# Linear attention, then a squared-ReLU MLP, on one core: diagonal sums on VectorE and GpSimd, state terms as row tiles, another order

## The chip, the core and the metric

The kernel runs on one core of one Trainium2 chip. The core has a matrix engine (TensorE, PE in the profile; PEld are its weight loads), VectorE (DVE), ScalarE (ACT), GpSimd (POOL) and SyncE (SP, which here only issues DMAs). Matrix products land in PSUM, 8 banks of 128 x 512 f32; operands lie in SBUF. The metric is the device time of one execution in microseconds, the median of several runs.

## The reference

For 4 batches, 8 heads, 768 positions and a head size of 48:

```
for t in range(S):
    cur = einsum('bhd,bhe->bhde', u * k[t], v[t])
    y[t] = einsum('bhd,bhde->bhe', r[t], state + cur)
    state = w * state + einsum('bhd,bhe->bhde', k[t], v[t])
x = y.transpose(0, 2, 1, 3).reshape(3072, 384)
out = relu(x @ w_in) ** 2 @ w_out        # 384 -> 2048 -> 384
```

## The kernel before, in words

**Units.** The 768 positions are cut into 6 chunks of 128. A unit is one chunk of one batch, all 8 heads: 24 units, numbered so that units 4c to 4c + 3 are chunk c of the four batches. Heads go in 4 pairs; a pair is 2 x 48 columns, padded to 2 x 64 where it is turned.

**Attention of a unit.** `load` brings r, k and v (192 KB each, in `ldr`, `ldk`, `ldv`). `scale` (DVE) multiplies r with rising and k with falling powers of w into `rkw`, so that decay inside the chunk becomes a plain product. `turn` (PE, with `evict_rk` on ACT, units 0 to 5) or `turn_dma` (a DMA transpose, units 6 on) gives `rkT`. `at` computes k^T q for every head in two PSUM banks, the two heads of a pair on partitions 0 to 63 and 64 to 127 of the array; `ats` does it for two units (four banks). `mask` (DVE) applies the triangle and writes `am`. `y_mm` multiplies `am` with v (8 matmuls) and adds r times the state (4 matmuls with the state `stb`, in which the two heads of a pair stand in a block-diagonal 128 x 96 with zeros elsewhere). The position's own term, the sum over d of r u k, times v, is the diagonal: `rk` (DVE) multiplies the turned r and k, `sums` contracts the product with `uwb` on PE (4 matmuls of 8 columns), `diag_v` (DVE) multiplies the sums with v, and `evict_y` (DVE) adds that to y.

**State.** `sums` also forms k^T v (4 matmuls). `state_add` adds it to `st32`, `state_decay` multiplies with the decay of a chunk, both DVE; `state_cast` (ACT) writes the bf16 copy `stb`, in two halves. Chunk 5 needs no new state.

**MLP.** y goes turned (`x_turn` and `evict_x`, or `x_dma`) into `xT`; `mm1` computes a slice of the hidden layer for one or two units (12 or 6 matmuls), `relu` on ACT, `square` on ACT or DVE, `mm2` a quarter of the second product (4 matmuls of 384 columns), `evict_o` and `store`. The last unit's product goes in two halves (`mm2_half`).

**Order.** A text, `SCHEDULE`, lists every step; each engine works its own instructions in that order. `@` gives the PSUM banks that a step takes, `name:unit:...` its arguments; the last field of `square` is 1 for ACT and 0 for DVE; `load` and `store` name the queue. `fill` is a matmul on constants whose result nobody reads. `SP` also issues both kinds of transposing DMA.

Lines that are named below: 233 fill, 288 scale, 311 turn, 320 rk, 328 at, 340 mask, 348 diagonal sums, 353 state sums, 362 diag_v, 370 to 376 state, 382 state_cast, 391 and 397 y, 406 evict_y, 421 x_turn, 435 mm1, 443 relu, 452 and 454 square, 461 mm2, 476 halves, 260 the small chain of products on GpSimd in the head.

Of the kernel before, what the change touches and what calls it, by code (L numbers as in the profile page):

```python
# [26 lines left out]
2*fill:256@7 fill:256@2 evict_y:0 fill:256@2 wout:1:0 mm1:1:1:1@7 state_add:0 x_turn:0@2 load:4:kt:POOL mm1:1:1:0@6  # L27
mask:2:1 evict_x:0 relu:1:1:1 state_add:1 mm1:0:1:0@3 relu:1:1:0 mm1:0:1:1@1 mask:2:0 square:1:1:1:1 scale:3:1
relu:0:1:0 4*fill:256@7 square:1:1:0:0 fill:256@7 cast_v:2 3*fill:256@7 state_cast:1 fill:256@7 square:0:1:0:0
sums:2@2 wout:2:0 y_mm:2@0 mm1:0:1:2@7 relu:0:1:1 diag_v:2 evict_y:2 mm1:1:1:2@4 load:4:vt:POOL load:6:kt:SP scale:3:0  # L30
x_turn:2@6 turn:3:1@5 state_add:2 evict_x:2 turn:3:0@3 fill:256@0 evict_rk:3:1 fill:256@0 square:0:1:1:0 mm1:2:1:2@1
evict_rk:3:0 wout:3:0 mm1:2:1:0@0 relu:1:1:2 rk:3 relu:0:1:2 at:3@6,2 load:5:vt:POOL relu:2:1:0 mm1:2:1:1@5 mask:3:1
cast_v:3 mm1:1:1:3@3 square:2:1:0:0 relu:2:1:1 mask:3:0 mm1:2:1:3@4 square:1:1:2:1 square:2:1:1:1 mm1:0:1:3@7
scale:4:0 relu:2:1:2 mm2:1:0@0 relu:1:1:3 scale:5:0 sums:3@2 relu:0:1:3 y_mm:3@5 turn:4:0@6 diag_v:3 square:2:1:2:1
mm2:0:0@1 square:0:1:2:1 evict_y:3 mm2:2:0@3 state_add:3 evict_rk:4:0 mm2:1:1 state_cast:0 scale:4:1 x_turn:3@7
square:0:1:3:0 relu:2:1:3 mm2:0:1 evict_x:3 square:1:1:3:0 turn:4:1@5 mm2:2:1 evict_rk:4:1 load:9:kt:SP mm1:3:1:1@6
cast_v:4 rk:4 at:4@2,4 relu:3:1:1 load:7:kt:SP mm1:3:1:0@7 mask:4:1 square:2:1:3:1 mm2:1:2 mask:4:0 relu:3:1:0
# [10 lines left out]
relu:5:1:3 load:8:vt:SP evict_o:2 sums:7@0 mask:7:0 load:11:kt:SP mm2:4:1 relu:5:1:1 rk:8 load:11:rt:SP store:2:POOL
relu:5:1:2 mm2:4:2 diag_v:7 store:3:POOL state_add:7 y_mm:7@1 store:0:POOL mm2:4:3 scale:10:1 store:1:POOL mm1:6:1:0@7
evict_y:7 square:5:1:2:0 x_dma:7 mm1:6:1:1@3 relu:6:1:0 state_decay:7 mm2:5:0@4 square:5:1:1:0 square:6:1:0:1  # L50
load:11:vt:SP square:5:1:3:1 ats:8@6,5,0,1 load:12:kt:SP relu:6:1:1 mm2:6:0@7 mask:8:0 mm1:6:1:3@3 rk:9 scale:10:0
mm1:6:1:2@6 mask:9:0 relu:6:1:3 turn_dma:10 mm2:5:1 mask:9:1 relu:6:1:2 sums:9@3 cast_v:8 mask:8:1 y_mm:9@0
# [20 lines left out]
mask:14:0 load:18:kt:SP mm2:10:3 mask:15:1 mm1:12:2:3@5 mask:14:1 turn_dma:16 mask:15:0 mm1:12:2:1@6 relu:12:2:3
scale:17:0 mm1:12:2:5@7 cast_v:15 load:16:vt:SP scale:17:1 square:12:2:3:1 mm1:12:2:0@4 turn_dma:17 mm2:11:2
relu:12:2:0 y_mm:15@3 relu:12:2:5 load:17:vt:SP sums:15@5 relu:12:2:1 sums:14@4 state_add:15 mm1:12:2:7@7
square:12:2:1:1 diag_v:14 mm1:12:2:2@6 evict_o:8 diag_v:15 square:12:2:0:1 mm1:12:2:6@0 relu:12:2:7 evict_y:15
# [41 lines left out]
def kernel(  # L118
# [13 lines left out]
    C = 128  # L132
# [148 lines left out]
    def pair(x):  # L281
        return x.rearrange("p (a o) d -> p a o d", o=2)
# [263 lines left out]
```

## Time and profile before

| | |
|---|---|
| median of 3 runs | 173.61 us (173.19 to 174.07) |
| the execution profiled | 173.05 us, of which the span 171.3 |
| PE busy | 164.8 us (96%), 1931 matmuls |
| DVE busy | 138.0 us (81%) |
| ACT busy | 120.8 us (71%) |
| POOL busy | 30.5 us (18%), nearly all issuing DMAs |

The span is what the instructions cover; the rest of a time lies around it. A matmul's record is longer than its share of the pipeline (an `mm2` matmul shows 326 ns and the next starts 163 ns later), so PE work is read here from starts, in the chain of waits. Rows of a group read: line, engine, operation, output and input, count, then busy time and mean ns of one, then idle time before them. Rows of a timeline or chain begin with start and length in us.

### The profile page before, as it was taken

How to read it: one execution, taken by the hardware profiler on the slowest of the kernel's cores; microseconds unless marked ns; L12 is line 12 of the kernel's file. 1: busy time of each engine (PE TensorE's matmuls, PEld its weight loads, DVE VectorE, ACT ScalarE, POOL GpSimd, SP SyncE). 2: the span in 40 equal slices, each digit the busy share in tenths (PEclk: the TensorE clock that was granted, in tenths of full speed). 3: DMA queues.
4: the chain of work that ended last, by engine and by line, in shares of the span. 5: the costliest groups of instructions: out<-in, count | busy, mean ns of one | idle time of the engine just before them, and what ended most of it. 6: DMA issues, size and time to landing. Idle time of an engine off the chain costs nothing.

```text
span 171.3 us, 4810 instructions
## 1 busy us (share of the span) xinstructions
PE 164.8 (96%) x1931; PEld 132.1 (77%) x1931; DVE 138.0 (81%) x298; ACT 120.8 (71%) x252; POOL 30.5 (18%) x62
## 2 busy tenths in 40 slices
PE   7949999999999999999999999999999999999993
PEld 3637998787887788697796896896898776999662
DVE  5457997879999999999989879988989797764800
ACT  4533669999699547788599599499359986295830
POOL 8989440000002200000300000303000030030010
PEclk9987999999999999999999999999999999999999
DMA  5999999989996999899999999999959994150014
GB/s 106 199 212 213 220 249 244 222 157 158 187 169 120 286 145 169 166 186 148 238 229 123 182 186 128 254 149 204 262 97 211 201 150 134 32 161 0 4 62 168
DMA packets 94784, 28.83 MB, mean 168 GB/s; under 512 B 90665, under 2 KB 92714, under 8 KB 94762
## 3 DMA queue, kind: packets, MB, share of 16 engines
q1 hardware_dynamic: 90512, 19.08, 71.8%
q0 software_dynamic: 4224, 9.44, 21.1%
q8 instruction: 15, 0.25, 0.6%
q14 instruction: 7, 0.06, 0.1%
q10 hardware_dynamic: 26, 0.00, 0.0%
HBM read 20.45 MB, written 4.72 MB: 147 GB/s over the span
## 4 chain that ended last, share of the span: by engine, by line
PE 87%; DVE 5%; DMA 4%; POOL 2%; issue 1%; POOLq 0%; DVEq 0%
PE bank L461 35%; PE bank L435 35%; DMA ldr<-in_r_dram 4%; PE bank L328 4%; PE bank L391 3%; PE bank L353 2%; PE bank L397 2%; PE bank L476 2%; PE bank L233 1%; PE bank L311 1%; PE bank L348 1%; DVE yb L406 1%; DVE am L340 1%; DVE st L370 1%; PE bank L421 1%
## 5 line engine op out<-in xcount | busy, mean ns | idle before, releaser
L443 ACT ACTIVATE gr<-bank 128x512 f32<-128x512 f32 x96 | 53.8, 603 | 27.8 <-PE bank L435 24.4
L435 PE MATMUL bank<-xT,w_in_q 128*128 128x128 bf16 (+1 forms) x768 | 70.6, 246 | 0.0
L461 PE MATMUL bank<-w_out_q,g 128*128 128x384 bf16 x368 | 67.6, 326 | 0.0
L435 PEld LDWEIGHTS <-w_in_q 128*128 128x128 bf16 x768 | 64.1, 113 | 2.4
L461 PEld LDWEIGHTS <-g 128*128 128x128 bf16 x368 | 34.0, 98 | 18.9 <-ACT g L452 0.5
L454 DVE TENSOR_TENSOR g<-gr 128x512 bf16<-128x512 f32 x50 | 33.0, 686 | 6.5 <-ACT gr L443 6.4
L495 POOL DMA_DIRECT2D out_dram<-osb x21 | 11.3, 543 | 130.3 <-ACT osb L468 119.6
L340 DVE TENSOR_TENSOR am<-bank,smask 128x512 bf16<-128x512 f32 x48 | 30.8, 684 | 3.5 <-PE bank L328 3.2
L452 ACT ACTIVATE g<-gr 128x512 bf16<-128x512 f32 x46 | 28.2, 633 | 0.5
L406 DVE TENSOR_TENSOR yb<-bank,dv 128x384 bf16<-128x384 f32 x24 | 13.3, 556 | 3.9 <-PE bank L391 1.2
L288 DVE TENSOR_TENSOR rkw<-ldr,wpos 128x384 bf16<-128x384 f32 x24 | 12.9, 552 | 3.8 <-ACT wpos L241 2.2
L382 ACT CAST stb<-st 64x192 bf16<-64x192 f32 x40 | 13.9, 348 | 2.2 <-DVE st L376 1.9
L362 DVE TENSOR_TENSOR dv<-vb,bank 128x384 f32<-128x384 bf16 x24 | 13.0, 549 | 2.9 <-PE bank L353 2.1
L288 DVE TENSOR_TENSOR rkw<-ldk,wneg 128x384 bf16<-128x384 f32 x24 | 13.1, 552 | 0.6 <-DMA ldk<-in_k_dram 0.5
L292 ACT CAST vb<-ldv 128x384 bf16<-128x384 f32 x24 | 12.2, 512 | 0.6 <-DMA ldv<-in_v_dram 0.4
L468 ACT COPY osb<-bank 128x384 f32<-128x384 f32 x23 | 10.6, 481 | 2.7 <-PE bank L461 2.7
L372 DVE TENSOR_TENSOR st<-bank,st 64x192 f32<-64x192 f32 x32 | 11.3, 352 | 1.3 <-PE bank L353 1.0
L320 DVE TENSOR_TENSOR rk<-rkT 128x512 bf16<-128x512 bf16 x24 | 10.1, 419 | 1.9 <-ACT rkT L315 1.4
L233 PE MATMUL bank<-warm 128*128 128x256 bf16 x53 | 10.0, 336 | 1.2 <-DVE warm L179 1.2
L315 ACT COPY rkT<-bank 128x512 bf16<-128x512 bf16 x12 | 6.6, 591 | 4.1 <-PE bank L311 4.0
L328 PEld LDWEIGHTS <-rkT 64*128 64x128 bf16 x192 | 5.6, 95 | 4.6 <-issue 4.4
L328 PE MATMUL bank<-rkT 64*128 64x128 bf16 x192 | 8.1, 220 | 0.8 <-ACT rkT L315 0.8
(58 smaller groups left out, 112.6 us busy)
## 6 DMA issues: line engine op xcount, KB each, us to landing
ldk<-in_k_dram SPq DMA_DIRECT2D x22, 192.0 KB, 4.3
out_dram<-osb POOLq DMA_DIRECT2D x21, 192.0 KB, 3.5
ldr<-in_r_dram SPq DMA_DIRECT2D x20, 192.0 KB, 4.3
ldv<-in_v_dram SPq DMA_DIRECT2D x19, 192.0 KB, 4.5
w_in_q<-in_moe_w_in_dram POOLq DMA_DIRECT2D x4, 384.0 KB, 9.6
w_out_q<-in_moe_w_out_dram POOLq DMA_DIRECT2D x4, 384.0 KB, 10.8
ldv<-in_v_dram POOLq DMA_DIRECT2D x5, 192.0 KB, 9.6
ldr<-in_r_dram POOLq DMA_DIRECT2D x4, 192.0 KB, 8.9
```

Of the source, the lines that this page charges most:

```text
L288: nc.vector.tensor_tensor(t["rkw"][:, x, :, :, :D], pair(src), pair(wx), ALU.mult)
L292: nc.scalar.copy(tiles[i]["vb"], tiles[i]["vt"])
L328: nc.tensor.matmul(out=t["at"][o][:, p, :], lhsT=t["rkT"][sl, 1, p, :], rhs=t["rkT"][sl, 0, p, :], start=True, stop=True,)
L340: nc.vector.tensor_tensor(am, t["at"][o], smask.unsqueeze(1).to_broadcast([C, HP, C]), ALU.mult)
L362: nc.vector.tensor_tensor(t["dv"], t["vb"], t["d"].unsqueeze(2).to_broadcast([C, H, D]), ALU.mult)
L382: nc.scalar.copy(stb[b][sl, :, o * D : (o + 1) * D], st32[b][sl])
L406: nc.vector.tensor_tensor(t["yb"], t["y"], t["dv"].rearrange("p h d -> p (h d)"), ALU.add)
L435: nc.tensor.matmul(out=t["h", s][:, a], lhsT=turned, rhs=chunks[c]["xT"][:, n, b : b + m, :], start=(n == 0), stop=(n == NK - 1),)
L443: nc.scalar.activation(t["gr", s], t["h", s], AF.Relu)
L452: nc.scalar.activation(g, x, AF.Square)
L454: nc.vector.tensor_tensor(g, x, x, ALU.mult)
L461: nc.tensor.matmul(out=t["o"], lhsT=chunks[units[i][0]]["g"][:, f, units[i][1], :], rhs=w_out_q[f // 4][:, f % 4, :], start=(f == 0), stop ...
```

## The change

From unit 8 on, three things are computed in another way, and the whole order is another one.

1. **Diagonal sums.** Instead of `rk` and 4 matmuls, `product` (DVE) multiplies r and k before they are turned, `weigh` (POOL) multiplies by w u, laid out over all partitions by two loads and one product that stand around the steps of units 7 and 8, two `fold`s (POOL) add halves of the 48 columns to 24 and 12, and `head_sums` (DVE) reduces the last 12.
2. **y from the state.** `ats` is followed by 8 matmuls per unit, one a head, with 64 rows each, that use the state as it is (`stc`, one cast from unit 4 on) and write each head's half of y: one bank for the even heads of both units, one for the odd. `ys` later adds `am` times v for both units.
3. **evict_y** reads the two banks, in two instructions.

```
+    def wide_load(x):
+        src = (w, u)[x].rearrange("h d -> (h d)").unsqueeze(0).to_broadcast([128, dm])
+        nc.sync.dma_start(out=wide[x].rearrange("p h d -> p (h d)"), in_=src)
+    def wide_product():
+        nc.gpsimd.tensor_tensor(wide[1], wide[1], wide[0], ALU.mult)
+    def product(i):
+        t["pr"] = buffer("pr", [C, H, D], BF16)
+        nc.vector.tensor_tensor(pair(t["pr"]), t["rkw"][:, 0, :, :, :D], t["rkw"][:, 1, :, :, :D], ALU.mult)
+    def weigh(i):
+        t["pw"] = buffer("pw", [C, H, D], F32)
+        nc.gpsimd.tensor_tensor(t["pw"], t["pr"], wide[1], ALU.mult)
+    def fold(i, n):
+        x = tiles[i]["pw"]
+        m = D >> (n + 1)
+        nc.gpsimd.tensor_tensor(x[:, :, :m], x[:, :, :m], x[:, :, m : 2 * m], ALU.add)
+    def head_sums(i):
+        t["d"] = buffer("ds", [C, H], F32)
+        nc.vector.tensor_reduce(out=t["d"], in_=t["pw"][:, :, : D // 4], axis=mybir.AxisListType.X, op=ALU.add)
+    def halves(i):
+        return [bank("y", i - i % 2, o).rearrange("p (u x) -> p u x", u=2)[:, i % 2, : dm // 2].rearrange("p (a d) -> p a d", a=HP) for o in range(2)]
     def ats(i):
         at(i)
         at(i + 1)
+        for j in (i, i + 1):
+            y = halves(j)
+            for p in range(HP):
+                for o in range(2):
+                    sl = slice(o * 64, o * 64 + 64)
+                    nc.tensor.matmul(
+                        out=y[o][:, p, :], lhsT=tiles[j]["rkT"][sl, 0, p, :], rhs=stc[units[j][1]][sl, p, :],
+                        start=(j == i and p == 0), stop=False, skip_group_check=True,
+                    )
...
-        for p in range(HP):
+        for p in range(HP if i < WIDE_FROM else 0):
...
-        for o in range(2):
+        if i >= WIDE_FROM - B:
+            nc.scalar.copy(stc[b], st32[b])
+        for o in range(2 if i < WIDE_FROM - B else 0):
...
+    def ys(i):
+        for j in (i, i + 1):
+            for p in range(HP):
+                for o in range(2):
+                    nc.tensor.matmul(
+                        out=y[o][:, p, :], lhsT=t[f"am{o}"][:, p, :], rhs=t["vb"][:, 2 * p + o, :],
+                        start=False, stop=j > i and p == HP - 1, skip_group_check=True,
+                    )
...
+        if i >= WIDE_FROM:
+            for o, y in enumerate(halves(i)):
+                nc.vector.tensor_tensor(out_y[:, o], y, dv[:, o], ALU.add)
+            return
```

The order, from its start to the first `mm1` step, before and after:

```
-load:1:kt:SP fill:256@7 load:0:rt:SP 2*fill:256@7 load:0:kt:SP 2*fill:256@7 load:1:rt:POOL 2*fill:256@7 load:2:kt:SP
-2*fill:256@7 columns:0 columns:1 load:1:vt:POOL spread_log@0 load:2:vt:SP load:2:rt:POOL load:5:rt:SP fill:256@7
-power:0 win:0:0 2*fill:256@7 power:1 fill:256@7 scale:0:0 fill:256@7 load:0:vt:POOL fill:256@7 scale:1:1 2*fill:256@7
-turn:1:1@1 win:1:0 scale:0:1 turn:0:0@2 evict_rk:1:1 load:3:kt:POOL scale:1:0 turn:0:1@3 load:5:kt:SP evict_rk:0:0
-turn:1:0@4 evict_rk:0:1 win:2:0 spread_columns@5 evict_rk:1:0 rk:0 load:3:rt:POOL cast_v:1 rk:1 at:1@6,7 copy_columns
-at:0@0,1 u_columns scale:2:0 fill:256@5 scale:2:1 fill:256@5 end_columns turn:2:0@2 fill:256@5 mask:0:0 turn:2:1@3
-evict_rk:2:0 sums:1@4 mask:0:1 evict_rk:2:1 3*fill:256@5 2*fill:256@2 mask:1:0 at:2@5,0 win:3:0 2*fill:256@3 mask:1:1
-2*fill:256@3 fill:256@6 cast_v:0 load:3:vt:POOL 2*fill:256@6 diag_v:1 fill:256@6 y_mm:1@2 y_mm:0@3 load:6:rt:SP
-sums:0@1 evict_y:1 wout:0:0 2*fill:256@7 rk:2 fill:256@7 load:4:rt:POOL x_turn:1@6 diag_v:0 2*fill:256@7 evict_x:1
...
+load:0:rt:SP fill@7 load:1:kt:SP 3*fill@7 load:0:kt:SP load:1:rt:POOL load:2:kt:SP columns:0 columns:1 load:2:rt:POOL
+spread_log@0 load:2:vt:SP load:1:vt:POOL load:5:rt:SP fill@7 power:1 win:1:0 power:0 load:0:vt:POOL scale:0:0
+scale:1:1 win:0:0 load:5:kt:SP turn:1:1@1 load:3:kt:POOL scale:0:1 turn:0:1@2 win:2:0 turn:0:0@3 evict_rk:0:1 fill@0
+load:3:rt:POOL fill@0 evict_rk:1:1 fill@0 scale:2:0 fill@2 evict_rk:0:0 fill@2 scale:1:0 spread_columns@4 scale:2:1
+fill@3 rk:0 turn:2:0@5 turn:1:0@6 2*fill@3 evict_rk:1:0 fill@3 at:0@7,0 evict_rk:2:0 rk:1 at:1@2,1 mask:0:0 cast_v:1
+turn:2:1@3 fill@6 fill@5 evict_rk:2:1 fill@5 copy_columns mask:0:1 u_columns at:2@6,5 mask:1:1 win:3:0 cast_v:0
+sums:1@7 mask:1:0 cast_v:2 end_columns diag_v:1 y_mm:1@4 sums:0@3 rk:2 y_mm:0@0 evict_y:1 diag_v:0 x_turn:1@1 fill@4
...
```

One stretch of the steady part, after:

```
+store:7:POOL evict_o:6 square:8:2:4:0 load:15:vt:SP ats:12@6,0,1,4,3,2 square:8:2:5:0 scale:15:1 mm2:9:2 mask:12:0
+weigh:13 turn_dma:15 mm2:8:2 mask:13:1 mm1:10:2:0@6 fold:13:0 load:16:kt:SP scale:14:0 mm1:10:2:4@4 relu:10:2:0
+fold:12:0 mask:12:1 square:8:2:6:1 mm1:10:2:5@6 turn_dma:14 fold:12:1 mask:13:0 relu:10:2:4 store:5:POOL mm1:10:2:3@0
+head_sums:12 square:8:2:7:1 state_decay:11 fold:13:1 mm1:10:2:1@1 cast_v:13 load:17:rt:SP head_sums:13 product:14
+mm1:10:2:7@4 diag_v:12 relu:10:2:1 state_decay:10 ys:12 square:10:2:0:1 diag_v:13 mm2:8:3 state_cast:11 evict_y:12
```

The new order has 14 fills between the first `mm1` and the steps of unit 10, and one in the tail; the old one has 11 after the first `mm1`, all before unit 4. Squares: 50 on DVE and 46 on ACT before, 37 and 59 after.

More of the change, by code (lines that the diff above doesn't have):

```diff
@@ L28 @@
[L28 to L37, printed above, removed]
@@ L48 @@
[L48 to L52, printed above, removed]
@@ L73 @@
[L73 to L76, printed above, removed]
-mm1:12:2:4@5 relu:12:2:2 state_decay:12 x_dma:15 square:12:2:7:0 y_mm:14@7 square:12:2:2:1 mm2:13:0@3 evict_y:14
@@ new lines @@
+ats:10@6,7,0,3,1,5 product:11 square:7:1:2:1 fold:10:1 load:14:kt:SP cast_v:11 store:4:POOL mm2:6:3 mask:11:0
+load:12:vt:SP state_cast:8 weigh:11 state_cast:9 mask:10:1 mm2:7:1 load:15:rt:SP mask:10:0 mm2:7:2 fold:11:0
+load:15:kt:SP mask:11:1 mm2:7:3 fold:11:1 scale:13:1 mm1:8:2:0@0 head_sums:11 turn_dma:13 product:13 mm1:8:2:3@7
+head_sums:10 relu:8:2:0 scale:12:1 fill@3 mm1:8:2:1@6 scale:12:0 relu:8:2:3 square:8:2:0:0 turn_dma:12 fill@0
+sums:11@3 relu:8:2:1 ys:10 diag_v:10 fill@7 square:8:2:3:1 mm1:8:2:5@0 evict_y:10 square:8:2:1:1 load:14:rt:SP
```

170 lines of the change are left out of this document (99 added, 71 removed).

## The prediction

> **What bounds the kernel now.** I read the chain of waits first, then the busy time by stage, then the timeline of the first 18 us.
>
> ```profile
> span 171.3 us, 4810 instructions
> PE 87%; DVE 5%; DMA 4%; POOL 2%; issue 1%; POOLq 0%; DVEq 0%
> ```
>
> TensorE (PE) is 87% of the chain. The same chain in order of time gives the pitch of each kind of matmul, from one start to the next; the unit steps are these.
>
> ```profile
> 24.75 0.22 PE bank L233 x2
> 35.09 0.33 PE bank L328 x8
> 35.42 0.79 PE bank L435 x12
> 36.87 0.22 PE bank L311 x4
> 37.09 0.67 PE bank L435 x12
> 37.76 0.65 PE bank L461 x4
> 38.41 0.08 PE bank L348 x4
> 38.49 0.19 PE bank L353 x4
> 38.68 0.20 PE bank L391 x8
> 38.88 0.17 PE bank L397 x4
> 42.22 0.27 PE bank L421 x3
> 96.11 2.62 PE bank L435 x24
> 118.92 0.55 PE bank L328 x16
> 119.47 1.41 PE bank L461 x8
> 165.83 2.65 PE bank L476 x32
> ```
>
> The row-tiled `at` matmuls delay what follows: 0.79 instead of 0.67, and 1.41 instead of 1.30, so 8 cost 0.45 and 16 cost 0.66. Summed over the order: 32 `mm1` of one unit x 0.67 = 21.4, 64 of two units x 0.655 = 41.9, 92 `mm2` x 0.65 = 59.8, the halves 2.65, 8 single `at` 3.6, 8 paired 5.3, state sums 20 x 0.19, diagonals 24 x 0.08, `y_mm` 24 x 0.20 and 20 x 0.17, 12 turns 2.6, 6 x-turns 1.6: **152.9 us of useful PE work**. PE ends at 165.83 + 2.65 = 168.5, so it idles or runs fills (dummy matmuls) for 15.6 us in all.
>
> ```profile
> 82.30:94.20 11.90, 11.90 (x136) 9.62 (x138) 10.74 (x23) 9.69 (x21) 0.72 (x2) 1.00 1.09 196
> sum 109.80, PE 109.77 PEld 88.54 DVE 90.39 ACT 79.11 POOL 9.11; mean PE 12.20 PEld 9.84 DVE 10.04 ACT 8.79 POOL 1.01
> ```
>
> This view by stage (columns: length, PE, PEld, DVE, ACT, POOL) covers 58.7, the start of `ats:8`, to 168.5: 109.8 us, where my sum of useful steps is 109.5. So from unit 8 on PE waits for practically nothing, and VectorE (DVE) is at 90% in the stretch quoted. All but 0.3 us of the 15.6 lies before 58.7, and 14.0 of it before the first `mm1` at 17.88 (done by then: 6 turns, 3 `at`, 2 sums, 2 y, one x-turn, 3.9 us).
>
> ```profile
> 2.23 1.06 POOL L267 DMA_DIRECT2D ldr<-in_r_dram  x1
> 3.29 0.90 POOL L267 DMA_DIRECT2D ldv<-in_v_dram  x1
> 4.17 0.88 POOL L267 DMA_DIRECT2D ldr<-in_r_dram  x1
> 5.38 0.57 ACT L241 ACTIVATE wneg<-bank,down 128x384 f32<-128x384 f32 x1
> 5.51 0.56 DVE L288 TENSOR_TENSOR rkw<-ldr,wpos 128x384 bf16<-128x384 f32 x1 [2.18 <-ACT wpos L241]
> 7.15 0.56 DVE L288 TENSOR_TENSOR rkw<-ldr,wpos 128x384 bf16<-128x384 f32 x1
> 11.28 0.56 DVE L288 TENSOR_TENSOR rkw<-ldr,wpos 128x384 bf16<-128x384 f32 x1 [1.45 <-DMA ldr<-in_r_dram]
> 12.23 2.48 DVE L340 TENSOR_TENSOR am<-bank,smask 128x512 bf16<-128x512 f32 x4
> 15.02 1.05 PE L233 MATMUL bank<-warm 128*128 128x256 bf16 x8
> 15.91 0.56 PE L391 MATMUL bank<-vb,am 128*128 128x48 bf16 x16
> 16.36 0.56 DVE L406 TENSOR_TENSOR yb<-bank,dv 128x384 bf16<-128x384 f32 x1 [1.20 <-PE bank L391]
> 17.88 0.83 PE L435 MATMUL bank<-xT,w_in_q 128*128 128x128 bf16 x12
> 12.00:14.00 2.00, 2.00 (x20) 1.75 (x20) 2.00 (x4) 1.17 (x2) 1.74 (x6) 0.50 1.19 238
> ```
>
> In the head DVE stands at `scale:2:0` until r of unit 2, third on POOL's queue, lands at 11.28; the four masks of units 0 and 1 queue behind it until 12.23. Then 8 fills from 15.02 hold `y_mm:1` and `evict_y:1` back. The granted clock (third column from the end) is 0.50 after a pause.
>
> **The change, part by part.** *PE, units 8 to 23.* Removed: diagonals 0.08 and y from the state 0.17, 16 x 0.25 = 4.0 us. Added: 8 row-tiled matmuls of 48 columns per unit. Eight more `at` matmuls of 128 columns cost 0.55 - 0.33 = 0.22, four pairs at 55 ns, so pairs do overlap. Bounds per unit: 0.08 (scaled by columns) and 0.22 (as if 128). I take 0.16, the diagonals' 20 ns per matmul, which have hardly a column and so show the weights' price: 2.6 us. Net **-1.4 us** (-2.7 to -0.5); useful work 151.5. `ys` joins the same 16 matmuls, 0.40: nothing.
>
> *DVE.* For its operations the page has (and, last, a load of 192 KB and its 4.3 us to landing):
>
> ```profile
> L454 DVE TENSOR_TENSOR g<-gr 128x512 bf16<-128x512 f32 x50 | 33.0, 686 | 6.5 <-ACT gr L443 6.4
> L406 DVE TENSOR_TENSOR yb<-bank,dv 128x384 bf16<-128x384 f32 x24 | 13.3, 556 | 3.9 <-PE bank L391 1.2
> L382 ACT CAST stb<-st 64x192 bf16<-64x192 f32 x40 | 13.9, 348 | 2.2 <-DVE st L376 1.9
> L320 DVE TENSOR_TENSOR rk<-rkT 128x512 bf16<-128x512 bf16 x24 | 10.1, 419 | 1.9 <-ACT rkT L315 1.4
> ldk<-in_k_dram SPq DMA_DIRECT2D x22, 192.0 KB, 4.3
> ```
>
> 512 against 384 elements is about 1.02 ns an element and 0.16 us fixed; all-bf16 goes at half that. Per unit: `rk` -0.42, `product` +0.35 (0.56 if its strided rows lose the bf16 rate), `head_sums` of 96 elements +0.26, `evict_y` as two halves of 192 instead of one, 0.71 - 0.56 = +0.15. That is +0.34, times 16 = +5.4. The orders have 50 squares on DVE before and 37 after: -13 x 0.69 = -8.9, which ACT takes in exchange for half of its 32 casts from unit 4 on (-16 x 0.35 = -5.6); ACT has 30 us of room in the 109.8. Measured DVE busy over the sum of its durations is 90.39 / 100.5 = 0.90, since neighbours overlap. With it, the new stretches from `ats:8` to `ats:22` and on to the first `mm1:20` have, PE then DVE: 7.3/7.2, 12.2/11.1, 12.2/11.8, 12.9/11.8, 10.9/10.1, 18.1/15.9, 7.9/6.5, 2.3/1.3. DVE fits in each, with 8.1 us of room in sum and 0.1 to 2.2 in each.
>
> *POOL.* 16 times `weigh` (384 elements) and two folds (192 and 96), not shown before at this size. Nearest rows:
>
> ```profile
> masks.py:65 POOL MEMSET smask<- 128x128 f32 x1 | 0.2, 204 | 0.0
> L530 POOL MEMSET const-float32-1.0<- 128x1 f32 x1 | 0.1, 99 | 0.0
> L260 POOL TENSOR_TENSOR wend_c<-wend_c x6: 198/198/522, 11.1 to 13.0; 128x4 f32<-128x4 f32 x6
> ```
>
> One pass over an element is (204 - 99) / 127 = 0.83 ns, the fixed part 0.20 us. Two reads and a write cost between one pass and three (0.83 to 2.5 ns); I take two, 1.7: 672 x 1.7 ns + 0.6 = 1.75 us a unit, 28 us in all (1.16 to 2.28 a unit). The stretches last 12 us for two units, so POOL has time. What matters is the last row's maximum: one of six equal operations took 0.52 instead of 0.20, while DVE ran the scale of 11.28, whose two inputs lie in SBUF; those that ran beside the masks (one input in PSUM) kept 0.198. So the two engines block each other here, and the new POOL work may hold DVE. About half of DVE's steady work reads two SBUF tensors (scale, square, product, diag_v, decay): 28 us x 1/2 = 14 us held if each hit costs the whole operation, 7 if half of it on average, 0 if DVE always goes first. I take 7, since the order puts most folds beside masks. Spread evenly, 0.9 a stretch, it overruns the room by 0.8 and 0.5 in the first and third: **+1.0 us** (0 to 6.4).
> The Trainium skill, "SBUF — State Buffer", section "SBUF: two separate sides", speaks against the change: whichever of a DVE operation with two SBUF inputs and a GpSimd operation starts first keeps the shared port pair for its whole length, and the other blocks fully. The 0.52 us agrees for GpSimd's side; no row shows DVE's. By "GPSIMD Engine Reference", "Performance versus the Vector engine" (2.6 cycles of 1.2 GHz for a two-input element), the estimate is 2.1 us a unit, 33 us.
>
> *Head.* r of unit 2 moves to second place on POOL's queue. POOL's loads land one after another: the first by 7.15, the third at 11.28, so the second at about 9.2. `power:1` first makes `wpos` late (5.9). Then DVE: three scales to 7.5, `scale:2:0` 9.2, `scale:1:0`, `scale:2:1`, two `rk` to 11.6, masks 11.6 to 14.2 with a copy between, `diag_v:1` to 14.7, `evict_y:1` to 15.2 (no fills in front of `y_mm:1`), and as before 17.88 - 16.36 - 0.56 = 0.96 to the first `mm1`: 16.1. By then 4.2 us of useful work are done (one more sum), so the slack is 11.9 instead of 14.0: **-2.1 us** (-2.5 to +0.5). v of unit 1, now third, lands by 11.3, before its cast is needed.
>
> *After the head.* Before, 1.3 us of slack: 11 fills of 0.11. The new order has 14 (units 1 to 10; the last one in the tail is free), 1.5 us, and I leave 0.3 for waits: **+0.5 us** (0 to 2). The two wide loads on SP (192 KB each) are issued with five `mm2` and two `mm1` steps and six fills, over 5 us of PE work, between the first and `wide_product`, against 4.3 us to land; if they come later, POOL and `head_sums:9` wait once, up to 1 us. The stores keep POOL's queue, now behind `weigh` and `fold`, and four buffers cover them. Six banks instead of four held by `ats` until the masks are covered by the two `mm2` pieces that stand behind it (1.3 us against 2.48 / 4 = 0.62 for a mask); without them PE would wait half a microsecond a pair. The tail's 32 halves stay.
>
> Sum: the execution profiled took 173.05 (span 171.3 and 1.75 around it); -1.4 - 2.1 + 0.5 + 1.0 gives 171.05. The median of the runs shown is 0.56 above it: **171.6 us**.
>
> **The rivals.**
> 1. *POOL holds DVE for its whole length* (slower). Place: from `ats:8`, DVE's scales, squares and products behind `weigh` and `fold`. Price: 14 us, 1.75 a stretch, exceeding the room by 6.4 instead of 1.0: 177.0. It decides from about 9.5 us held. For it: 0.52 against 0.198, and DVE at 90%. Against: folds stand beside masks.
> 2. *The head gains nothing*: r of unit 2 lands at 11.3 from second place too, since all loads share the DMA engines, or the fewer fills (18 instead of 42 before the first `mm1`) leave PE at the clock of 0.50: 171.6 + 2.1 = 173.7.
> 3. *POOL is late.* At 2.5 ns, `weigh:13` and four folds are 3.4 us plus a store of 0.5, between `mask:12:0` and `head_sums:13`, where DVE has 3.5 of its own; DVE, which is in order, waits 0.4 a pair, with the diagonals, y and x behind: 8 x 0.4 in place of the room left, 174.5.
> 4. *The row tiles do not overlap* (the change doesn't do what it says): 8 x 55 ns = 0.44 a unit instead of 0.16, +4.5: 176.1. The 0.55 for 16 speaks against it.
>
> **How the numbers follow.** Forecast 0.51, rival 1 0.20, rival 2 0.15, rival 3 0.11, rival 4 0.03. A measurement here tells 0.5%, 0.9 us, from no change. Faster: the forecast and a fifth of rival 2, 0.54. Same: most of rival 2, a third of rival 3, 0.15. Slower: the rest, 0.31. The forecast's own range is 169.8 to 172.7 (the bounds of PE and head); to hold 8 in 10 it must reach most of rival 1: 169.6 to 176.8.
>
> **What would show it.** Right: first `mm1` near 16; L348 with 32 matmuls; a paired `at` with its state matmuls near 0.87 us; stretches equal to their PE sums; `head_sums` waiting little on POOL; POOL operations near 0.85, 0.5 and 0.35. Wrong: scale, square or product durations well above 0.55, 0.69 and 0.35, idle DVE before `head_sums` ended by POOL, or PE waiting on masks in the stretches from unit 8; then the result is over 174.

## The result and the profile after

| | before | after |
|---|---|---|
| median | 173.84 us (4 runs) | 178.17 us (175.32 to 182.15, 4 runs) |
| ratio to the kernel before | | 1.012, 95% interval [1.0071, 1.0169] |
| the same, timed again | 173.93 us (13 runs) | 177.89 us, 1.0208 [1.014, 1.0276] |
| the execution profiled | 173.05 us, span 171.3 | 179.72 us, span 177.9 |

The change made the kernel 1 to 2% slower; the forecast was 1.2% faster. The ratio leaves out the two slow executions of the four, 179.72 us, which is the one profiled, and 182.15 us, so it rests on two and is below the ratio of the medians; what is read from this profile is therefore held against a second one, of 178.13 us (span 176.4). The first rows of the page of the changed kernel (busy time by engine) and the shares of its chain of waits:

```profile
span 177.9 us, 4860 instructions
PE 162.5 (91%) x1911; PEld 128.5 (72%) x1911; DVE 140.1 (79%) x317; ACT 120.4 (68%) x249; POOL 67.0 (38%) x111
PE 57%; DVE 18%; DMA 17%; SPq 3%; issue 2%; ACT 1%; DVEq 0%
```

TensorE's share of the chain fell from 87% to 57%; VectorE has 18% and DMA 17%. Of these 17%, 14 are one load, k of unit 5, which the chain follows back to 6.7 us although TensorE worked beside it; in the second profile, where that load came in time, TensorE has 74%. TensorE has less work than before and a longer span. Where it idles is seen in the view by stage, of the changed kernel first, then of the kernel before (stretch, length, PE, PEld, DVE, ACT, POOL busy, granted clock, DMA share, GB/s):

```profile
18.00:58.70 40.70, 37.88 (x540) 30.72 (x537) 31.30 (x66) 32.43 (x69) 6.47 (x10) 0.96 1.03 188
58.70:101.00 42.30, 38.27 (x467) 30.15 (x466) 39.89 (x85) 27.61 (x58) 20.95 (x29) 1.00 1.02 180
101.00:175.00 74.00, 73.80 (x783) 59.28 (x781) 57.06 (x128) 52.48 (x108) 26.23 (x40) 1.00 0.70 140
```

```profile
18.00:58.70 40.70, 40.57 (x602) 33.49 (x602) 36.35 (x76) 34.07 (x73) 5.45 (x9) 1.00 1.06 197
58.70:94.20 35.50, 35.50 (x432) 28.36 (x434) 33.35 (x71) 27.29 (x59) 1.60 (x3) 1.00 1.14 182
94.20:168.50 74.30, 74.27 (x776) 60.18 (x772) 57.03 (x113) 51.83 (x110) 7.50 (x14) 1.00 0.77 146
```

Before, TensorE idles 0.1 us of 40.7 and then not at all. After, it idles 2.8 us from 18 to 58.7 and 4.0 from 58.7 to 101 (1.5 and 4.6 in the second profile), where `ats:14` stands in the new order; from there on it is full again, although GpSimd works there too (26 us of 74, against 21 of 42). So the loss has a place: the stretch in which the transfers are dense (DMA share above 1) and VectorE is fullest (39.9 us busy of 42.3), not the whole steady part. The old kernel is as dense and as full there (1.14, and 33.4 of 35.5) and loses nothing, so that alone does not explain the loss. The chain of waits of the changed kernel, in order of time (start, length, what), names the stalls:

```profile
6.69 25.73 DMA ldk<-in_k_dram
...
32.45 0.57 DVE rkw L296
...
33.07 0.50 PE bank L319 x4
33.56 1.28 PE bank L528 x4
...
72.81 4.51 DMA xT<-yb
...
77.46 1.47 PE bank L502 x12
...
86.12 2.81 DVE g L521 x2
...
97.49 2.94 DVE g L521 x3
...
100.47 1.47 PE bank L528 x8
101.95 0.55 PE bank L363 x16
102.50 0.20 PE bank L379 x16
102.70 1.41 PE bank L528 x8
```

Three kinds of stall: a scale that stands in VectorE's order ahead of its load (k of unit 5 lands at 32.4; TensorE waits 3.0 us for the turn behind it, and after this pause four `mm2` matmuls take 1.28 us instead of 0.65: the granted clock was 0.50 from 33.2 to 36.6 us), a transpose of x that takes 4.5 us, and squares (L521): two in 2.81 and three in 2.94 us. The last rows are a gain: the row tiles (L379) take 0.20 us for two units.

To compare kernels by place I use the prediction's slack: the start of a step on TensorE less the useful TensorE work before it by the prediction's pitches (row tiles at 0.10 us a unit, as just read). The last column goes by the end of the span, less the 2.9 us by which the old kernel's outlasts TensorE.

| slack of TensorE, us, at | first `mm1` | `ats:8` | `ats:14` | end |
|---|---|---|---|---|
| before | 14.0 | 15.2 | 15.4 | 15.5 |
| after | 13.0 | 18.7 | 24.1 | 24.5 |
| after, second profile | 12.6 | 17.4 | 22.7 | 23.0 |

Useful work fell from 152.9 to 150.5 us and slack grew by 9.0 (7.5 in the second profile). Less 2.4, that is the 6.6 us by which the span grew.

### The profile page after: what moved, and what is told of

It reads as the page before. It is cut to its first block, busy times and chain, and to the rows that moved or that the text cites. A ratio compares the mean times of both kernels' runs of the same rounds, so it can differ in the third digit from the quotient of the medians.

```text
span 177.9 us, 4860 instructions
## 1 busy us (share of the span) xinstructions
PE 162.5 (91%) x1911; PEld 128.5 (72%) x1911; DVE 140.1 (79%) x317; ACT 120.4 (68%) x249; POOL 67.0 (38%) x111
## 4 chain that ended last, share of the span: by engine, by line
PE 57%; DVE 18%; DMA 17%; SPq 3%; issue 2%; ACT 1%; DVEq 0%
PE bank L502 25%; PE bank L528 23%; DMA ldk<-in_k_dram 14%; DVE g L521 4%; DVE am L387 4%; SPq L275 3%; DVE rkw L296 3%; DMA xT<-yb 3%; PE bank L363 2%; DVE st L424 2%; PE bank L543 1%; DVE st L420 1%; DVE dv L410 1%; PE bank L440 1%; DVE yb L471 1%
## 5 line engine op out<-in xcount | busy, mean ns | idle before, releaser
L528 PE MATMUL bank<-w_out_q,g 128*128 128x384 bf16 x368 | 68.6, 328 | 2.3 <-DVE g L521 2.2
L510 ACT ACTIVATE gr<-bank 128x512 f32<-128x512 f32 x96 | 54.8, 606 | 22.6 <-PE bank L502 21.8
L519 ACT ACTIVATE g<-gr 128x512 bf16<-128x512 f32 x59 | 36.8, 642 | 0.3
L521 DVE TENSOR_TENSOR g<-gr 128x512 bf16<-128x512 f32 x37 | 27.4, 762 | 9.4 <-ACT gr L510 9.3
L340 POOL TENSOR_TENSOR pw<-pr,wide 128x384 f32<-128x384 bf16 x16 | 17.0, 1068 | 45.7 <-DVE pr L335 45.7
L562 POOL DMA_DIRECT2D out_dram<-osb x21 | 11.8, 565 | 44.4 <-ACT osb L535 35.1
L345 POOL TENSOR_TENSOR pw<-pw 128x192 f32<-128x192 f32 (+1 forms) x32 | 19.3, 615 | 1.3
L471 DVE TENSOR_TENSOR yb<-bank,dv 128x192 bf16<-128x192 f32 x32 | 9.7, 350 | 1.4 <-PE bank L440 1.2
L410 DVE TENSOR_TENSOR dv<-vb,ds 128x384 f32<-128x384 bf16 x16 | 9.7, 619 | 0.1
L319 PE MATMUL bank<-identb,rkw 128*128 128x128 bf16 x48 | 5.5, 270 | 4.7 <-DVE rkw L296 4.7
L241 PE MATMUL bank<-warm 128*128 128x256 bf16 x33 | 8.6, 338 | 1.2 <-DVE warm L184 1.2
```

Source lines behind the costliest of these rows:

```text
L340: nc.gpsimd.tensor_tensor(t["pw"], t["pr"], wide[1], ALU.mult)
L345: nc.gpsimd.tensor_tensor(x[:, :, :m], x[:, :, :m], x[:, :, m : 2 * m], ALU.add)
L510: nc.scalar.activation(t["gr", s], t["h", s], AF.Relu)
L519: nc.scalar.activation(g, x, AF.Square)
L521: nc.vector.tensor_tensor(g, x, x, ALU.mult)
L528: nc.tensor.matmul(out=t["o"], lhsT=chunks[units[i][0]]["g"][:, f, units[i][1], :], rhs=w_out_q[f // 4][:, f % 4, :], start=(f == 0), stop ...
```

## The experiments

**Three edits that take one thing away.** The changed kernel itself again; `scale:5:1`, its turn and its eviction moved behind unit 4's; GpSimd's arithmetic left out (`weigh`, `fold` and `wide_product`, so that `head_sums` adds unweighted products and the diagonal sums are not the reference's); both.

```
-square:2:1:2:1 turn:4:1@0 scale:5:1 mm2:1:0@5
+square:2:1:2:1 turn:4:1@0 mm2:1:0@5
...
+scale:5:1 evict_rk:4:0
...
-        nc.gpsimd.tensor_tensor(t["pw"], t["pr"], wide[1], ALU.mult)
+        return
```

> The changed kernel once more. Theory A (k of unit 5 lands near 32.4 us, and the new order has its scale on VectorE near 29): the stall of 3 us at 33 us stands in this trace too, time 175 to 177. Theory B (GpSimd's weigh and fold hold VectorE): squares near 760 ns and state_decay near 500 again, PE gaps of 4 to 5 us in sum between 77 and 101. Theory C (neither; the order itself packs too much on VectorE and the DMA queue around units 7 to 9): gaps there, whatever the durations.

> scale, turn and evict_rk of k of unit 5 moved some 3 us down, behind the landing at 32.4. A: the PE gap of 3.0 at 33 us shrinks below 1, the clock stays at 1.00 from 30 to 40, time down 3 to 4: 172 to 173. B and C: the time won there is lost again at 77 to 100, where VectorE is behind: 174.5 to 176.

> Leaves out wide_product, weigh and fold; head_sums reduces 12 columns of product instead, so the diagonal sums are not the reference's. Everything else, the order too, stays. B: squares back at 686 ns, state_decay at 352, diag_v at 549, the gaps between 77 and 101 vanish, time down 4 to 5: 171 to 172. A: the stall at 33 stays and is all that matters, time as of the changed kernel, 175 to 176. C: durations fall but the gaps at 77 to 101 stay, less than 1.5 saved.

> Both edits: GpSimd's weigh and fold left out (diagonal sums not the reference's) and k of unit 5 later. A with B: the two add up, 168 to 169.5. A alone: 172 to 173, as with the later scale alone. B alone: 171 to 172. C: over 173.

Measured: again 1.0208 [1.014, 1.0276]; `scale:5:1` later 1.0129 [1.0074, 1.0183]; no GpSimd arithmetic 1.0089 [1.0043, 1.0136]; both 1.0113 [1.0062, 1.0165]. With the early scale in place GpSimd's part is 1.2% of the time (0.3% by the first ratio, 1.012); with the scale later it is 0.2%, and there the intervals overlap. So these runs do not settle its price in this order. The early scale's part is not settled either: the intervals overlap, and in the second profile of the changed kernel k of unit 5 landed at 29.0 us, in time, and the stall at 33 us was not there; instead TensorE waited 1.1 and 1.9 us, at 46.7 and 63.8 us, for turned r and k. And the two don't add up: without both, something else still costs 1.1%.

**GpSimd's work, and mere GpSimd activity, in the old kernel.** Nothing of the change but GpSimd operations of the sizes of `weigh` and `fold`, unused, from unit 8 on; then memsets that keep GpSimd busy as long and read nothing.

```
+        nc.gpsimd.tensor_tensor(pair(t["pw"]), t["rkw"][:, 1, :, :, :D], pair(wneg), ALU.mult)
...
+        nc.gpsimd.tensor_tensor(x[:, :, :m], x[:, :, :m], x[:, :, m : 2 * m], ALU.add)
```

> The kernel before, with one weigh and two folds a unit from unit 8 on added on GpSimd, whose result nobody uses (the output stays the reference's). It measures the hold by itself, in an order that left PE no gap. B (GpSimd's operations hold VectorE): squares, scales and state_decay grow by 50 to 150 ns in the mean, 6 to 8 us held in sum; VectorE has some 16 us of room from unit 8 on in the old order, so the time grows by 1 to 4, to 175 to 177. If the hold is only of GpSimd, durations stay and the time is 173.9.

```
+        t["pw"] = buffer("pw", [C, 1024], F32)
+        nc.gpsimd.memset(t["pw"], 0.0)
...
+        nc.gpsimd.memset(x[:, : (640, 480)[n]], 0.0)
```

> The kernel before with GpSimd memsets of about 0.95, 0.63 and 0.5 us a unit from unit 8 on, in the places where the run with weigh and folds had its reads; a memset reads no SBUF. Theory (GpSimd holds VectorE by sharing its way to SBUF for two-input operations, so what counts is the reads, not that GpSimd is busy): squares stay at 0.69 us, scales near 0.55, rk near 0.42, time within 0.5% of before, 173.0 to 174.8. Rival (any GpSimd work as long holds VectorE, its writes too): squares near 0.74, rk near 0.6 and 179 to 182 as with weigh and folds. A mixture would be squares near 0.71 and 175 to 177.

Measured: 181.56 us, 1.0441 [1.0394, 1.0487] with the reads, where 175 to 177 was expected; 173.65 us, 0.9943 [0.99, 0.9985] with the memsets. The groups of costliest instructions (count, then busy us, mean ns) of the run with reads:

```profile
L467 DVE TENSOR_TENSOR g<-gr 128x512 bf16<-128x512 f32 x50 | 36.0, 744 | 6.3 <-ACT gr L456 6.2
L353 DVE TENSOR_TENSOR am<-bank,smask 128x512 bf16<-128x512 f32 x48 | 30.8, 683 | 2.2 <-PE bank L341 1.9
L291 DVE TENSOR_TENSOR rkw<-ldk,wneg 128x384 bf16<-128x384 f32 x24 | 15.2, 638 | 0.8 <-DMA ldk<-in_k_dram 0.7
L333 DVE TENSOR_TENSOR rk<-rkT 128x512 bf16<-128x512 bf16 x24 | 14.3, 595 | 1.3 <-ACT rkT L318 1.1
L323 POOL TENSOR_TENSOR pw<-rkw,wneg 128x384 f32<-128x384 bf16 x16 | 15.5, 967 | 35.2 <-DVE rkw L291 35.1
```

and of the run with memsets:

```profile
L466 DVE TENSOR_TENSOR g<-gr 128x512 bf16<-128x512 f32 x50 | 33.0, 685 | 6.3 <-ACT gr L455 6.2
L352 DVE TENSOR_TENSOR am<-bank,smask 128x512 bf16<-128x512 f32 x48 | 30.8, 683 | 3.6 <-PE bank L340 3.2
L291 DVE TENSOR_TENSOR rkw<-ldk,wneg 128x384 bf16<-128x384 f32 x24 | 13.2, 552 | 1.4 <-DMA ldk<-in_k_dram 1.3
L332 DVE TENSOR_TENSOR rk<-rkT 128x512 bf16<-128x512 bf16 x24 | 10.0, 419 | 1.8 <-ACT rkT L318 1.1 <-DMA rkT<-rkw 0.4
L388 DVE TENSOR_TENSOR st<-st,wend_c 128x192 f32<-128x192 f32 x16 | 5.6, 351 | 0.1
L323 POOL MEMSET pw<- 128x1024 f32 x16 | 15.4, 965 | 0.0
```

Beside GpSimd's reads every VectorE operation with both inputs in SBUF is longer (square 744 for 685 ns, scale of k 638 for 552, `rk` 595 for 419), and the mask, with one input in PSUM, is not (683 in both). Beside memsets of like length (965 ns against 967, the shorter ones 632 and 498 against 727 and 568) nothing is longer. This is shown: what holds VectorE is that both engines read SBUF, not that GpSimd is busy. The Trainium skill states just this ("SBUF — State Buffer", section "Who interferes with whom": a VectorE instruction with two SBUF inputs contends with a GpSimd instruction that reads SBUF, not with one that only writes it); the runs agree. The price in the old kernel, whose VectorE has no more room than its stretches show, is 7.7 us. The same groups in the changed kernel:

```profile
L387 DVE TENSOR_TENSOR am<-bank,smask 128x512 bf16<-128x512 f32 x48 | 30.9, 684 | 6.9 <-PE bank L363 6.7
L521 DVE TENSOR_TENSOR g<-gr 128x512 bf16<-128x512 f32 x37 | 27.4, 762 | 9.4 <-ACT gr L510 9.3
L296 DVE TENSOR_TENSOR rkw<-ldk,wneg 128x384 bf16<-128x384 f32 x24 | 14.0, 595 | 3.3 <-DMA ldk<-in_k_dram 3.1
L424 DVE TENSOR_TENSOR st<-st,wend_c 128x192 f32<-128x192 f32 x16 | 8.0, 505 | 0.1
L335 DVE TENSOR_TENSOR pr<-rkw 128x384 bf16<-128x384 bf16 x16 | 5.6, 349 | 0.0
L350 DVE TENSOR_REDUCE ds<-pw 128x8 f32<-128x96 f32 x16 | 3.7, 244 | 0.0
L340 POOL TENSOR_TENSOR pw<-pr,wide 128x384 f32<-128x384 bf16 x16 | 17.0, 1068 | 45.7 <-DVE pr L335 45.7
L345 POOL TENSOR_TENSOR pw<-pw 128x192 f32<-128x192 f32 x16 | 11.8, 744 | 0.8
L345 POOL TENSOR_TENSOR pw<-pw 128x96 f32<-128x96 f32 x16 | 7.6, 487 | 0.5
```

By these means VectorE is held 37 x (762 - 685) = 2.8 us in squares, 24 x (595 - 552) = 1.0 in scales of k and 16 x (505 - 351) = 2.5 in decays, and some 1.9 more in scales of r and `diag_v`: about 8 us.

**Parts of the change in other surroundings.** The diagonal sums by VectorE and GpSimd alone in the old order; and the other way round, the changed kernel with the diagonals back on TensorE (row tiles, `ys` and the new order kept, scale of unit 5 later). In two of these runs, pe_diag and pe_diag_loads, the sums of odd units share columns with y, so their values are not the reference's; pe_diag_loads also moves the loads that stand shortly ahead of a transpose of x behind it, and pe_diag_early moves only `load:14:rt`, ahead of `load:15:rt`.

```
-rk:8
+weigh:8 fold:8:0 fold:8:1
...
-diag_v:8
+head_sums:8 diag_v:8
```

> Part 1 of the change alone (product, weigh, fold, head_sums from unit 8 on) in the old order; y from the state and the rest as before. PE loses 64 small matmuls, 1.3 us. B: the hold costs more than that, 174 to 176. C (the new order is the loss): 172.5 to 173.5.

> The changed kernel with k of unit 5 later and the diagonal sums on PE again (rk on VectorE, 4 matmuls a unit into a free corner of y's bank); no GpSimd arithmetic, no wide loads; row tiles, ys and the new order stay. Useful PE work 151.8. B: no gap over 0.7 us between 77 and 101, 171 to 172. D (in the new order the transposing DMAs land late, since they share SyncE's queue with loads): gaps that a transpose ends, 2 to 4 us in sum between 60 and 95, 173.5 to 175.5.

> The same, with each load that stood within 30 steps ahead of an x_dma on SyncE's queue moved behind it. D: the x transposes land earlier, 1.5 to 3 us less than pe_diag. B and C: the same as pe_diag within 0.5, or later where a load comes late.

> The changed kernel without GpSimd's arithmetic: diagonals on TensorE as before, with the row tiles and the new order kept, scale:5:1 later, and load:14:rt issued before load:15:rt instead of right ahead of the transposes of x of units 10 and 11. Theory (what is left over at 86 us is the x transposes that queue behind that load): they land 1 to 2 us sooner, the gap of 2.6 us at 86 us shrinks below 1.5, and the time falls from 175.7 to 174.0 to 175.0. Rival (the order has too many transfers in this stretch, wherever the load stands): a gap of the same size there or beside it, 175.3 to 176.5.

Measured: before_diag 189.19 us, 1.0845 [1.0771, 1.092]; pe_diag 175.67, 1.011 [1.0061, 1.0158]; pe_diag_loads 181.46, 1.0438 [1.0384, 1.0492]; pe_diag_early 176.19, 1.0108 [1.0079, 1.0137]. GpSimd's way cannot be put into the old order as it stands: there `head_sums` waits 2.9 us for GpSimd and `mm1` 3.2 for masks behind it. Without it the new order is still 1.1% slow. In pe_diag the largest stall was a transpose of x that took 6.88 us, to 86.1 us. Moving one load away from it removed that stall and not the time, which came back in stalls of 0.2 to 0.6 us; holding all loads back made it worse. So that stall alone was not the cause, and my expectation of pe_diag_early missed.

**The two wide loads.** They are the only transfers that the change adds. First they alone go into the old kernel, on SP ahead of `turn_dma:9`, unused. Then they are taken away: w u is multiplied in one row of 384 in the head and spread over the partitions by one matmul with ones, as the logarithm of w already is, and copied out by ScalarE.

```
+        nc.vector.tensor_tensor(urow, urow, wrow, ALU.mult)
...
+        nc.tensor.matmul(out=spread["wide"], lhsT=ones, rhs=urow, start=True, stop=True)
...
+        nc.scalar.copy(wide[1].rearrange("p h d -> p (h d)"), spread["wide"])
```

> The kernel before with the two wide loads (192 KB each, unused) on SP ahead of turn_dma:9, and nothing else. Theory (SP's queue is so full from 40 to 100 us that two more transfers make the transposes behind them late): a gap of 1 to 2 us on TensorE between 58 and 75 us, ended by DMA xT or rkT, and 175.0 to 176.2 against 173.9. Rival (the transfers fit beside the others): no new gap over 0.5 us and a time within 0.5% of before.

> The changed kernel with scale:5:1, its turn and its eviction later, once more, for its profile beside the two that follow: near 176.4.

> The run without GpSimd's arithmetic and with scale:5:1 later (its diagonal sums are not the reference's), now also without the two wide loads: w*u comes from a row, spread by one matmul in the head. Theory (wide loads on SP): the gap of 1.8 us at 63 us goes, the later x transposes come sooner, 173.0 to 174.6 against 176.05. Rival (the order's other transfers are late by themselves): within 0.4% of 176.05.

> The changed kernel whole, with its GpSimd arithmetic, but with w*u spread from a row in the head instead of the two wide loads, and scale:5:1 later. Theory (two causes of like size, the wide loads and GpSimd's hold, each hidden in part by the other's stalls): 174.3 to 175.8, above both_row (174.1) by what GpSimd holds on the path, and below the run with the loads (176.3). Rival (the loads alone decide): within 0.3% of both_row.

Measured: the old kernel with the two loads 176.51 us, 1.0142 [1.0083, 1.0202]; both edits and no loads (diagonal sums again not the reference's) 174.11, 1.003 [0.9994, 1.0065]; the whole change with the scale later and no loads 175.16, 1.0105 [1.0071, 1.0139]. The run named k5_later_row is the one with the scale later once more, at 176.26. The chain of the old kernel with the two loads:

```profile
76.32 4.57 DMA rkT<-rkw
80.89 4.12 DMA xT<-yb
...
85.14 2.90 PE bank L440 x25
```

Two loads of 192 KB, issued at 52 us, cost the old kernel 1.4%, 2.5 us, and the largest stall is not where they are but 30 us later, at a transpose of x. In this stretch SP issues one DMA after another, each 0.4 to 3 us. Its transposes of x start 0.9 us earlier than in the old kernel ahead of the loads (50.1 for 51.0), and 0.6 to 1.3 us later behind them, up to 91 us. In the change's own order the loads cost less: 0.2% with GpSimd's arithmetic (1.0129 to 1.0105) and 0.8% without (1.0113 to 1.003), and in both pairs the intervals overlap. Without the loads, the new order with no GpSimd arithmetic is level with the old kernel (1.003), and with the arithmetic 0.75% above that, some 1.3 us. The two intervals, of separate measurements, just don't touch. So by the three pairs of runs GpSimd's price in the change's own order is 1.2%, 0.2% or 0.75%.

**The change from unit 14 on.** Old head, order and forms up to unit 13, the change's from unit 14, where its profile shows TensorE full; the wide loads on GpSimd's queue (hybrid), then w u from a row (hybrid_row, timed twice), then also `load:14:rt` behind two transposes of x (hybrid_row2).

```
-    WIDE_FROM = 8
+    WIDE_FROM = 14
...
+store:1:POOL wide_load:1:POOL wide_load:0:POOL
```

> Head, order and forms of the kernel before up to unit 13, and the change's forms and order (row tiles, diagonal sums by VectorE and GpSimd) from unit 14 on; the two wide loads go through GpSimd's queue at about 60 us. Theory (the change's own work is a gain where its order is dense; its loss comes from the stretches between the first mm1 and ats:14): TensorE's slack before ats:14 stays near 15.5 as in the kernel before, 0.5 at most is added after it, and ten units with 0.15 us less work each give 172.0 to 173.3. Rival (GpSimd holding VectorE costs the same per unit in the later stretches too, and only hides there in slack from earlier delays): 2 to 4 us of new gaps after ats:14, 175 to 178.

> The hybrid (old head, order and forms up to unit 13, the change's from unit 14) without the two wide loads: w*u is spread from one row by a matmul in the head. Theory (the hybrid's 1.2 us at 66 us and the lateness that SP carries on to 87 us come from the wide loads): both gaps go, slack at ats:14 back to 15.5 to 16, 172.0 to 173.5. Rival (GpSimd's hold and the new forms cost as much without them): 175 to 177 with the gaps at 87 and 114 us left.

> hybrid_row with load:14:rt issued behind the transposes of x of units 11 and 10 instead of ahead of turn_dma:13. Theory (that load, 192 KB, makes these transposes late): the gap of 1.3 us at 84.5 us falls below 0.5, 171.3 to 172.5 against 172.9. Rival (SP is behind there whatever this load does): a gap of the same size there or at 95 us, 172.6 to 173.5.

> hybrid_row once more, more often timed. Theory (0.15 us less work in each of ten units, and slack as before but for 1.3 us at 84.5): 0.990 to 0.997 of before again, 172.2 to 173.4. Rival (its ratio was a matter of that chip and call): 0.997 to 1.005.

Measured: hybrid 176.74 us, 1.0176 [1.011, 1.0243]; hybrid_row 172.89, 0.9938 [0.9908, 0.9967], and again 172.91, 0.9933 [0.9902, 0.9964]; hybrid_row2 1.0071 [1.0035, 1.0108]. The chain of the hybrid with the wide loads:

```profile
58.17 7.69 DMA xT<-yb
...
65.90 0.83 PE bank L502 x12
```

and of the one without:

```profile
79.94 4.42 DMA xT<-yb
...
84.50 1.58 PE bank L507 x13
```

With the loads in flight, issued on GpSimd's queue here, a transpose of x on SP's took 7.69 us; without them the stall at 66 us is gone, and 3.9 us of the time. So most of the hybrid's loss was the loads, and they delayed SP's transposes although they were not on SP's queue. hybrid_row beats the kernel before by 0.65%, measured twice. How much of that is its doing is less sure: the memset run, whose profile shows nothing changed, read 0.9943, and one load moved in hybrid_row2 gave 1.3% away.

| slack of TensorE, us, at | first `mm1` | `ats:8` | `ats:14` | end |
|---|---|---|---|---|
| scale later | 14.1 | 15.6 | 21.3 | 21.6 |
| no GpSimd arithmetic | 14.0 | 15.1 | 18.1 | 19.6 |
| both, no loads | 13.1 | 14.7 | 20.1 | 20.5 |
| whole change, scale later, no loads | 12.6 | 14.5 | 19.1 | 19.5 |
| hybrid_row | 13.5 | 14.7 | 16.2 | 17.2 |

The row of the whole change without loads and early scale says what remains: up to `ats:8` its slack is below the old kernel's (14.5 for 15.2), and between `ats:8` and `ats:14` it still loses 4.6 us. Most of that lies in one stretch, from `ats:12` to `ats:14`. Here it is in the changed kernel, then without the arithmetic, without the arithmetic and the early scale, and without these and the loads:

```profile
86.47:101.88 15.41, 12.77 (x137) 9.69 (x137) 15.29 (x29) 8.89 (x19) 9.51 (x13) 1.00 0.88 172
83.01:95.94 12.93, 12.43 (x137) 9.66 (x138) 12.02 (x29) 8.88 (x19) 1.72 (x4) 1.00 1.11 185
83.13:98.46 15.33, 12.37 (x137) 9.66 (x138) 11.90 (x29) 8.88 (x19) 1.59 (x4) 1.00 1.02 169
81.83:97.93 16.10, 13.86 (x137) 10.32 (x137) 11.90 (x29) 8.99 (x19) 1.59 (x4) 0.89 0.87 162
```

The squares in the first two of these, and a transpose of x in the third:

```profile
L521 DVE TENSOR_TENSOR g<-gr 128x512 bf16<-128x512 f32 x6 | 6.5, 1120 | 1.0 <-ACT gr L510 1.0
L517 DVE TENSOR_TENSOR g<-gr 128x512 bf16<-128x512 f32 x6 | 3.9, 683 | 1.3 <-ACT gr L506 1.3
81.72 6.44 DMA xT<-yb
```

For this stretch the prediction had 12.2 us of TensorE and 11.8 of VectorE. With the arithmetic it takes 15.4 us, VectorE is busy for 15.3 of them, and TensorE waits 2.6 us for squares and masks; this is so in all five profiles of this order that have the arithmetic, with the loads and without. Left out, the arithmetic gives VectorE 3.3 us back, and the stretch takes 12.9. So here the hold stands on the path. But in the other two runs without the arithmetic the stretch takes 15.3 and 16.1 us though VectorE has only 11.9: TensorE waits 2.9 us for the transpose, or 2.2 us for masks, after which the granted clock was 0.50 for 3.4 us (this execution took 175.66 us, 1.5 more than the median of its kernel). A late transpose can take the hold's place, then, which fits that leaving the arithmetic out gains so little in one pair and more in another. Another order of these steps was not tried.

## Why the prediction was wrong, step by step

- **The step that failed: POOL's +1.0 us, the hold spread evenly over the stretches, 0.9 us in each.** The prediction held VectorE for 7 us (8 measured) and let 8.1 us of "room" swallow nearly all of it. VectorE had that room in sum, but 3.3 us of VectorE's time were added by it in the stretch from `ats:12` to `ats:14`, where the room was 0.4: it took 15.4 us instead of 12.2 (12.9 without the arithmetic), and TensorE waited there for squares and masks. The mechanism was named and its sum was sized; spreading it evenly was the error. In the whole time it shows as 1.2%, 0.2% or 0.75%, since late transposes delay the same stretch without it. Rival 1, the slower one, had the cause right, though not its place: the hold cost next to nothing after `ats:14`. The prediction's own overruns, 0.8 and 0.5, also make 1.3 us and not 1.0.
- **After the head: +0.5, "up to 1 us" for the wide loads.** Mis-sized. From the first `mm1` to `ats:8` the forecast had 1.8 us of slack (1.3 and 0.5); the two profiles have 5.7 and 4.8, and the one with the scale later 1.5. For the wide loads I asked only whether they land before `wide_product`. What they cost is what queues and flows beside them: 2.5 us in the old kernel, 3.9 in the hybrid, 0.4 to 1.4 in the change's own order, where it is not clear of the intervals. A late landing was weighed for the loads themselves and not for the transposes behind them.
- **The scale of unit 5 ahead of its load** was not seen at all. The trace of before has that load issued at 6.6 us and landed at 32.8, and the new order uses it at 29. It landed at 32.4, 29.0 and 25.5 us in three profiles with this order (the change twice, and without the arithmetic), so the stall cost 3.0 us, and a granted clock of 0.50 for 3.4 us behind it, in one profile and nothing in the next.
- **PE units: -1.4.** Better than forecast: row tiles 0.10 us a unit instead of 0.16, so -2.4. Rival 4 is out.
- **VectorE's sizes.** `product` 0.349 us (0.35 forecast), `head_sums` 0.244 (0.26): right. Also right was that the mask isn't held.
- **GpSimd's sizes.** 1.07, 0.74 and 0.49 us against 0.85, 0.5 and 0.35: 2.3 us a unit, at the upper bound of 2.28. The estimate by the Trainium skill ("GPSIMD Engine Reference", "Performance versus the Vector engine"), 2.1, was nearer. `head_sums` never waited for GpSimd (idle before it 0.0), so rival 3 is out; GpSimd waited for `product` (45.7 us).
- **Head: -2.1.** Half of it, at most two thirds. `scale:2:0` started at 9.14 as forecast (9.2) and the granted clock was 1.00 over the first 18 us, so both of rival 2's reasons were wrong, but the first `mm1` came at 17.14, not 16.1:

```profile
9.14 1.03 DVE L296 TENSOR_TENSOR rkw<-ldr,wpos 128x384 bf16<-128x384 f32 x2 [1.71 <-DMA ldr<-in_r_dram]
11.73 0.42 DVE L355 TENSOR_TENSOR rk<-rkT 128x512 bf16<-128x512 bf16 x1 [0.75 <-ACT rkT L323]
15.29 0.42 DVE L355 TENSOR_TENSOR rk<-rkT 128x512 bf16<-128x512 bf16 x1
15.63 0.55 DVE L473 TENSOR_TENSOR yb<-bank,dv 128x384 bf16<-128x384 f32 x1
```

  `rk:1` waited for ScalarE's eviction (0.75) and `rk:2` stood ahead of `evict_y:1` (0.42); my chain had neither. Slack at the first `mm1` fell by 1.0 and 1.4 us in the two profiles of the change, and not at all in two runs with the same head (14.1 and 14.0).

**What stays open:** without the loads, GpSimd's arithmetic and the early scale the new order is only level with the old kernel (1.003), where the prediction's other terms (-1.4, -2.1 and +0.5) would have made it 3.0 us faster. The traces show single waits there, for a transpose of x or for masks, which differ from one profile to the next; no run with another order tells whether they can be had back. Nor is it settled what the hold and the loads each cost in this order, or how often k of unit 5 is late.

## What to carry to other kernels

GpSimd's reads of SBUF and VectorE's operations with two inputs there are one resource (squares of 744 ns beside reads, 685 beside memsets): charge each hold to the step that waits for it, at the stretch where VectorE is fullest, not to an average. A small constant that is loaded in a stretch dense with transfers costs what stands behind it (2.5 us in the old kernel); build it on chip from a row, in a stretch where an engine is idle. Before trusting an order, compare each use of a loaded tile with its landing in the old trace, with a margin for how much landings move from run to run (25.5 to 32.4 us here).

## What was not expected of the hardware

- Sixteen row-tiled matmuls of 48 columns took 0.20 us (L379 above), 12.5 ns a matmul, against 20 ns that the prediction took from the diagonals' full-height ones.
- Reads on GpSimd stretched `rk` most of all in the mean (419 to 595 ns), an all-bf16 operation; writes by memset of like length stretched nothing.
- A DMA transpose of one y tile took 2.3 to 7.7 us from its issue to landing between 45 and 110 us (2.4 to 5.9 in the old kernel), and with two added loads the largest stall came 30 us behind them.
- The memset run's interval excluded 1 although its profile shows VectorE's operations unchanged (0.9943 [0.99, 0.9985]): about half a per cent is what one such ratio can tell here.
